# Sink values built one operation a step, and a narrower first query block

## The chip, the cores and the metric

The kernel runs on one core of a Trainium2 chip. The metric is the device time of one execution in microseconds (us). Five engines work side by side, each through its own queue in order: TensorE (PE; its weight loads are listed as PEld), VectorE (DVE), ScalarE (ACT), GpSimd (POOL), and SyncE (SP), which here only issues DMAs.

## The reference

Attention with a sliding window and sinks over 4 sequences, 8 heads, 768 positions and 64 dimensions, followed by a two-layer network over all 3072 tokens:

```
scores = q @ k.T / sqrt(64)
keep   = (key < 4) | (0 <= query - key < 128)        # sinks, window
a      = softmax(where(keep, scores, -1e9));  out = a @ v
x      = out of all heads side by side                # 3072 x 512
h      = x @ w_in                                     # 512 x 2048
g      = max(h, 0) + log1p(exp(-|h|))                 # softplus
result = g @ w_out                                    # 3072 x 512
```

## The kernel before

**Tiling.** A chunk is 256 queries of one sequence, two query blocks of 128 (j = 0 and 1). Three chunks make a sequence, so there are 12 chunks; chunks 0, 3, 6 and 9 are the first of their sequence (`self.first`). For each head and query block the scores are taken against the key block before it, 8 sink keys and its own key block: 128 + 8 + 128 = 264 columns. A predicated copy on VectorE (line 242) then lays the own block's kept scores (key not above the query) over those of the block before, so that 136 columns are left, 128 window keys and 8 sinks, to which a mask is added (line 248) and the exponential is taken on ScalarE (line 249). The host writes the first key block twice, so that the first query block of a sequence finds its own block also where the block before would stand; for it the copy writes values over equal ones.

**Precision.** Chunks 0 and 1 multiply in float32 (`exact`, scores at line 226). From chunk 2 on each operand is split into a rounded part in float32r (`hi`, fp32r in the profile) and a remainder, and a product is two or three matmuls in that type: the scores are hi x hi (line 229) and hi x remainder (line 230). So do the network's up product (line 459, 24 matmuls per 256 hidden units) and its down product (lines 496 to 498).

**Sink values.** The weights of the 8 sink keys are multiplied with the sinks' values in one matmul per head (line 327). Its stationary operand `vs` is built on POOL once per sequence for each group of 4 heads: after a DMA of the raw values (`load_sinks`, tile `vsr`), one operation rounds them (`vsh`, line 151), one takes the remainder in place (line 152), and for each group two operations place the rounded part and the remainder through a mask (line 158, tile `vs`). Six operations per sequence.

**Order.** In the main function the order of all engines is the order in which the program is written. A start phase is listed by hand (`START`). Then a loop runs over steps i, one head of attention each: while head i of the attention is finished, scores of head i+4 are made (S), softmax (T) and normalisation (N) of head i+4 follow, q, k and v of later heads are loaded and split (L, G, p, q), and for the network of the chunk before, one slice of 256 hidden units goes through up (U), softplus (F), gate (P), residue (R, a step later) and down (D, E, two steps later). W makes the transposed weights of head i and rearranges them on POOL into `pt` (lines 308, 311); V is the values' matmuls (lines 327, 333), which read `pt`. The gate's copy is POOL's rounding of softplus into `gh` (line 52), after VectorE's sum `mt` (line 474). The order of the letters in a step:

```
for part in "JjGL" + c.STEADY[i % H == 0]:
Ctx.STEADY = ("kWUqpKSFTRDVPONE", "SWTkpUKERDNFPqVO")
```

J and j build the sink values of the first and the second group of heads. J comes two steps ahead of a chunk's first step (chunk k begins at step 8k), at the head of the step, with the DMA and four POOL operations; j comes in step 8k+1, also at the head, with two operations. They run for the first chunk of each sequence and for chunk 2, the first one in the split form.

Of the kernel before, what the change touches and what calls it, by code (L numbers as in the profile page):

```python
# [12 lines left out]
F32R = mybir.dt.float32r  # L13
# [7 lines left out]
B, H, S, D = 4, 8, 768, 64  # L21
DM, DFF = 512, 2048
P = 128
NB = S // P
NS = 8
KW = P + NS
CH = 2
# [9 lines left out]
BIG = 3.0e38  # L37
G = 4
ORDERED = {mybir.EngineType.PE, mybir.EngineType.SP}


class Ctx:
# [80 lines left out]
class _Attention:  # L123
# [16 lines left out]
    def sinks(self, g):  # L140

        c, nc, b = self.c, self.c.nc, self.b
        raw = c.vsr[b]
        if self.exact:
            c.vs[b, g] = c.lp.tile([P, G, D], F32, tag=f"vsf{g}", name=f"vsf{g}", bufs=1)
            nc.gpsimd.memset(c.vs[b, g][:], 0.0)
            self._place(c.vs[b, g][:64], raw[:64, g : g + 1], 64)
            return
        if g == 0:
            c.vsh[b] = c.lp.tile([P, 2, D], F32R, tag="vsh", name=f"vsh{b}", bufs=1)  # L150
            nc.gpsimd.tensor_scalar(c.vsh[b][:], raw[:], 1.0, 0.0, ALU.mult, ALU.add)
            nc.gpsimd.tensor_tensor(raw[:], raw[:], c.vsh[b][:], ALU.subtract)
        c.vs[b, g] = c.lp.tile([P, G, P], F32R, tag=f"vs{g}", name=f"vs{b}_{g}", bufs=1)
        for src, o in ((c.vsh[b], 0), (raw, D)):
            self._place(c.vs[b, g][:, :, o : o + D], src[:, g : g + 1], P)

    def _place(self, out, src, rows):
        self.c.nc.gpsimd.tensor_tensor(
# [57 lines left out]
    def scores(self, h):  # L216
        c, nc = self.c, self.c.nc
        ops = self.heads.pop(h)
        for j in range(CH):
            pool, tag = (c.ps_h, "h") if self.chunk == 0 and h % 2 else (c.ps_s, "s")  # L220
            s = pool.tile([P, 2 * P + NS], F32, tag=tag, name=f"s{self.chunk}_{h}_{j}")
            mv = slice(j * KW, j * KW + 2 * P + NS)
            st = slice(KC + j * P, KC + j * P + P)
            if self.exact:
                q, k = ops
                nc.tensor.matmul(s[:], q[:, j * P : j * P + P], k[:, mv], start=True, stop=True)  # L226
            else:
                hi, kl = ops
                nc.tensor.matmul(s[:], hi[:, st], hi[:, mv], start=True, stop=False)  # L229
                nc.tensor.matmul(s[:], hi[:, st], kl[:, mv], start=False, stop=True)  # L230
            self.s[h, j] = s

    def softmax(self, h):
        c, nc, chunk = self.c, self.c.nc, self.chunk
        g, hh = h // G, h % G
        if hh == 0:
            self.a[g] = c.ap.tile([P, G, CH, KW], F32, tag="a", name=f"a{chunk}_{g}")
            self.rc[g] = c.sp.tile([P, CH, G], F32, tag="rc", name=f"rc{chunk}_{g}")
        sm = c.sp.tile([P, CH], F32, tag="sm", name=f"sm{chunk}_{h}")
        self.sm[h] = sm  # L240
        for j in range(CH):
            nc.vector.copy_predicated(self.s[h, j][:, :P], c.diag[:], self.s[h, j][:, KW:])  # L242
        for j in range(CH):
            a = self.a[g][:, hh, j]
            k = (chunk * H + h) * CH + j
            nm = c.stats[:, k : k + 1]
            m = c.masks[min(self.i0 + j, 2)]
            nc.vector.tensor_tensor_reduce(a, self.s.pop((h, j))[:, :KW], m[:], -SCALE, BIG, ALU.add, ALU.min, nm)  # L248
            nc.scalar.activation(a, a, AF.Exp, bias=nm, scale=-1.0, accum_out=sm[:, j : j + 1])  # L249
# [260 lines left out]
def _fast(c):  # L510
# [5 lines left out]
    n = c.nchunks  # L516
    att = [_Attention(c, k) for k in range(n)]
# [24 lines left out]
    def stage(kind):  # L542
        def run(i):
            if not todo[kind]:
                return
            o, e = todo[kind][0]
            before = "acdl"["acdl".index(kind) - 1]
            while kind != "a" and todo[before] and todo[before][0][0] <= o:
                stage(before)(i)
            home = _turn(c.WM, o)  # L550
            if kind == "a":
                while any(u is c.upper[c.turn] for u in c.top.values()):
                    stage("c")(i)
            elif kind == "c" and home == "p":
                while sum(_turn(c.WM, k) == "p" for k, _ in todo["l"] if k < o) > 1:
                    stage("l")(i)
            todo[kind].pop(0)
            if kind == "a":
                _weight_top(c, e, _turn(c.WT, o))
            elif kind == "c":  # L560
                _weight_f32(c, e, home)
            elif kind == "d":
                _weight_high(c, e, engine(c.WH, o))
            else:
                _weight_low(c, e, _turn(c.WL, o) if home == "s" else "V")

        return run
# [11 lines left out]
    def sinks(g):  # L579
        def run(i):  # L580
            k = (i - g * G) // H
            if (i - g * G) % H == 0 and k < n and (att[k].first or k == c.EXACT):
                if g == 0 and k:
                    att[k].load_sinks()
                att[k].sinks(g)

        return run

    parts = {
        "S": (call(att, "scores"), G),  # L590
# [15 lines left out]
        "G": (call(att, "load_v", 2), 2),  # L606
        "L": (call(att, "load"), G + 2),
        "J": (sinks(0), 2),
        "j": (sinks(1), G - 1),
        "w": (dma, 0),  # L610
        **{kind: (stage(kind), 0) for kind in "acdl"},
    }
# [183 lines left out]
def _kernel(tc, a, out):  # L796
# [7 lines left out]
    with ExitStack() as keep:  # L804
        c.const = keep.enter_context(tc.tile_pool(name="const", bufs=1))
        c.wp = keep.enter_context(tc.tile_pool(name="wp", bufs=1))
        c.w, c.raw, c.top, c.word = {}, {}, {}, {}
        c.ident = c.const.tile([P, P], F32, name="ident")
        c.stats = c.const.tile([P, B * H * NB], F32, name="stats")
        c.room = c.const.tile([P, 2, 4 * FP], F32, name="room")  # L810
        nc.gpsimd.memset(c.room[:], 1.0)
        c.sk = c.const.tile([P, CT], F32R, name="sk")
        ones = c.room[:].rearrange("p a b -> p (a b)").unsqueeze(1).broadcast_to([P, CT // 64, 64])
        _zero(nc, c.sk[:].rearrange("p (a b) -> p a b", b=64), ones)
        with ExitStack() as st:
            pool = lambda n, bufs: st.enter_context(tc.tile_pool(name=n, bufs=bufs))
            psum = lambda n, bufs: st.enter_context(tc.tile_pool(name=n, bufs=bufs, space=bass.MemoryType.PSUM))
            c.xp, c.mp, c.stg = pool("xp", 2), pool("mp", 2), pool("stg", 4)
            c.lp, c.ap, c.sp = pool("lp", 2), pool("ap", 2), pool("sp", 2)
            c.ps_acc, c.ps_h = psum("ps_acc", 1), psum("ps_h", 2)  # L820
            c.ps_s, c.ps_t, c.ps_x = psum("ps_s", 2), psum("ps_t", 1), psum("ps_x", 1)
            with tc.manual_schedule(engines=ORDERED):
                _fast(c)
        ok = nc.values_load(c.flag[:1, :1], min_val=0, max_val=1)
        with tc.If(ok < 1):
            _general(c)
# [8 lines left out]
Ctx.WT = "PAAVVVVAVAAVAAAVAAAAAAAAAAAPAAAV"  # L835
Ctx.WH = "VAPAAVAAAAVPPAAAAVVAVAAAAAVAVAAA"
Ctx.WL = "PPPPPPPVPPVPPVPPVPVPPPPVVPVVPVPV"
Ctx.STEADY = ("kWUqpKSFTRDVPONE", "SWTkpUKERDNFPqVO")
Ctx.START = """
S0 G4 T0 w w S1 j4 T1 J0 w L8 w w S3 S2 N0 N1 T2 W0 L10 w N2 S4 T3 N3 a w T4 k0 a c K0 a S5 c W1 w w  # L840
d S6 V0 O0 l d V1 w c l T5 N4 W2 T6 d w a S7 c O1 W3 l N5 G6 N6 a T7 c V2 N7 a d S8 k4 a O2 W4 w T8
# [62 lines left out]
```

## Time and profile before

| what | us |
|---|---|
| median of 3 runs (730.6 to 734.53) | 733.28 |
| the profiled execution | 729.99 |
| its span | 728.3 |
| TensorE busy in it | 695.7 |
| VectorE busy | 551.4 |
| ScalarE busy | 453.0 |
| POOL busy | 396.2 |

The span runs from the first to the last instruction of the profiled execution; its own time is a little longer. Busy is the time in which at least one instruction of the engine was under way. Matmuls overlap, so their pace is read from one start to the next and not from their duration. In lists of instructions a row gives the start in us from the beginning of the span, the duration, the engine, the line, the operation, the tile written and those read, the shape, the count, and in brackets the idle time of the engine before it and what ended that. A row of groups gives, after the bar, busy us and mean ns, and after the next bar idle us and who ended it. A row of waits gives us in total, times, and the longest. A row of stretches gives the stretch and its length, then for each engine the busy us with the number of instructions, the granted TensorE clock, and the DMA share and rate.

### The profile page before, as it was taken

To read this page: it belongs to the slowest core of one execution; us is meant where nothing else is said; L and a number is where in the kernel's file an instruction comes from. 1 tells how busy PE (TensorE), PEld (TensorE's weight loads), DVE (VectorE), ACT (ScalarE), POOL (GpSimd) and SP (SyncE) were. 2 spreads that over 40 slices of the span, in tenths; PEclk is the share of its full clock that TensorE was granted. 3 is DMA by queue.
4 is the path that set the end of the run, shared out by engine and by line. 5 is a ranking of instruction groups with operands and counts; after the bars stand their busy time and mean duration, and the time that the engine had idled before them with its cause. 6 is when DMAs were issued, how large, how long until landed. Compare 5 with 4: busy or idle time off the path is not lost.

```text
span 728.3 us, 13870 instructions
## 1 busy us (share of the span) xinstructions
PE 695.7 (96%) x4465; PEld 619.4 (85%) x4465; DVE 551.4 (76%) x1628; ACT 453.0 (62%) x1122; POOL 396.2 (54%) x769
## 2 busy tenths in 40 slices
PE   4888899999999999999999999999999999999996
PEld 3566689989999989988899999998899899999995
DVE  5899997877887887886977887886887877754331
ACT  3687865656676666765766766665766766744431
POOL 5766475575655655664664654656555565553110
PEclk9899999999999999999999999999999999999999
DMA  8888511411321321321222221321312312100001
GB/s 298 298 270 263 162 52 39 128 48 45 99 68 49 107 68 49 108 67 45 82 67 68 78 77 54 91 74 50 92 46 77 95 51 78 59 13 1 30 1 34
DMA packets 41205, 63.37 MB, mean 87 GB/s; under 512 B 4644, under 2 KB 22692, under 8 KB 41124
## 3 DMA queue, kind: packets, MB, share of 16 engines
q1 hardware_dynamic: 36372, 45.63, 21.4%
q10 hardware_dynamic: 4752, 16.77, 6.7%
q8 instruction: 37, 0.61, 0.4%
q14 instruction: 44, 0.36, 0.2%
HBM read 56.09 MB, written 6.29 MB: 86 GB/s over the span
## 4 chain that ended last, share of the span: by engine, by line
PE 83%; DVE 7%; POOL 3%; ACT 3%; issue 1%; DMA 1%; ACTq 0%; SPq 0%; POOLq 0%; DVEq 0%
PE h L459 33%; PE acc L496 11%; PE acc L497 11%; PE acc L498 11%; PE x L333 6%; PE s L229 2%; PE t L297 2%; PE s L230 2%; PE x L327 2%; PE s L226 2%; ACT a L249 1%; DVE wt L403 1%; DVE s L242 1%; POOL a L263 1%; POOL pt L308 1%
## 5 line engine op out<-in xcount | busy, mean ns | idle before, releaser
L459 PE MATMUL h<-xh,wi 128*128 128x256 f32 x1536 | 253.4, 287 | 0.0
L459 PEld LDWEIGHTS h<-xh,wi 128*128 128x128 f32 x1536 | 210.9, 191 | 1.1 <-issue 0.3
L459 PE MATMUL h<-xl,wi 128*128 128x256 f32 x768 | 154.5, 283 | 0.0
L496 PE MATMUL acc<-wo,gh 128*128 128x512 f32 x384 | 152.8, 398 | 0.0
L498 PE MATMUL acc<-wo,gl 128*128 128x512 f32 x384 | 151.0, 393 | 0.9 <-DVE gl L56 0.9
L52 POOL TENSOR_SCALAR gh<-mt 128x512 fp32r<-128x512 f32 x91 | 56.9, 626 | 173.8 <-DVE mt L474 147.8
L497 PE MATMUL acc<-wo,gh 128*128 128x512 f32 x384 | 150.8, 393 | 0.0
L466 ACT ACTIVATE mt<-h 128x512 f32<-128x512 f32 x96 | 57.5, 599 | 104.0 <-PE h L459 103.5
L263 POOL TENSOR_SCALAR a<-a,rc 128x128 f32<-128x128 f32 x180 | 71.9, 412 | 91.2 <-DVE rc L256 47.7
L459 PEld LDWEIGHTS h<-xl,wi 128*128 128x128 f32 x768 | 119.4, 191 | 0.0
L474 DVE SCALAR_TENSOR_TENSOR mt<-h,mt 128x512 f32<-128x512 f32 x96 | 65.8, 685 | 47.2 <-ACT mt L468 34.6
L249 ACT ACTIVATE a<-a,stats 128x136 f32<-128x136 f32 x192 | 76.0, 397 | 38.5 <-DVE stats L248 38.5
L498 PEld LDWEIGHTS acc<-wo,gl 128*128 128x128 f32 x384 | 72.2, 188 | 17.8 <-DVE gl L56 1.3
L496 PEld LDWEIGHTS acc<-wo,gh 128*128 128x128 f32 x384 | 72.4, 189 | 12.9 <-issue 0.5
L497 PEld LDWEIGHTS acc<-wo,gh 128*128 128x128 f32 x384 | 72.4, 189 | 9.4
L56 DVE TENSOR_TENSOR gl<-mt,gh 128x512 fp32r<-128x512 f32 x96 | 72.9, 759 | 4.9 <-POOL gh L52 4.6
L468 ACT ACTIVATE mt<-mt 128x512 f32<-128x512 f32 x96 | 60.8, 633 | 3.1
L467 ACT ACTIVATE mt<-mt 128x512 f32<-128x512 f32 x96 | 60.7, 633 | 3.1
L48 ACT CAST qkh<-qk 128x656 fp32r<-128x656 f32 x80 | 59.3, 741 | 1.2 <-DMA qk<-qk 1.2
L242 DVE COPY_PREDICATED s<-diag,s 128x128 f32<-128x128 int32 x192 | 48.6, 289 | 14.5 <-PE s L230 11.3
L56 DVE TENSOR_TENSOR kl<-qk,qkh 128x400 fp32r<-128x400 f32 x80 | 52.3, 654 | 2.5
L333 PE MATMUL x<-pt,vv 128*128 128x256 f32 (+1 forms) x216 | 48.9, 328 | 4.7 <-POOL pt L311 4.7
(182 smaller groups left out, 1207.7 us busy)
## 6 DMA issues: line engine op xcount, KB each, us to landing
qk<-qk SPq DMA_DIRECT2D x160, 164.0 KB, 3.0
vr<-v SPq DMA_DIRECT2D x32, 192.0 KB, 2.7
out<-o SPq DMA_DIRECT2D x24, 256.0 KB, 2.1
q<-q SPq DMA_DIRECT2D x8, 256.0 KB, 4.9
vr<-v SPq DMA_DIRECT2D x16, 128.0 KB, 2.2
k<-k SPq DMA_DIRECT2D x8, 200.0 KB, 4.7
wi00r<-w ACTq DMA_DIRECT2D x1, 511.8 KB
wi01r<-w ACTq DMA_DIRECT2D x1, 511.8 KB
```

The source lines that it names most:

```text
L48: nc.scalar.copy(out, in_)
L56: (nc.vector if eng == "V" else nc.gpsimd).tensor_tensor(out, a, b, ALU.subtract)
L249: nc.scalar.activation(a, a, AF.Exp, bias=nm, scale=-1.0, accum_out=sm[:, j : j + 1])
L263: (nc.vector if eng == "V" else nc.gpsimd).tensor_scalar(a, a, rc[:, j : j + 1], 0.0, ALU.mult, ALU.add)
L333: nc.tensor.matmul(x[:, :, o], w, pt[:, :, m], start=False, stop=n == 2, skip_group_check=True)
L459: nc.tensor.matmul(h[:, j], wt, x, start=k == 0, stop=k >= len(prods) - 2, skip_group_check=True)
L467: nc.scalar.activation(t[:], t[:], AF.Exp, scale=-1.0)
L468: nc.scalar.activation(t[:], t[:], AF.Ln, bias=1.0)
L474: nc.vector.scalar_tensor_tensor(t[:], h[:], 0.0, t[:], ALU.max, ALU.add)
L496: nc.tensor.matmul(acc[:], gh[:, j, q], wh, start=f == 0, stop=False, skip_group_check=True)
L497: nc.tensor.matmul(acc[:], gh[:, j, q], wl, start=False, stop=False, skip_group_check=True)
L498: nc.tensor.matmul(acc[:], gl[:, j, q], wh, start=False, stop=f == 2 * FP - 1, skip_group_check=True)
```

## The change

**Sink values.** J and j stay for chunk 0 and chunk 2 alone. For chunks 3, 6 and 9 a new letter Y does the same work in single pieces, at a place behind q (the split of v) and ahead of P (the gate): in step 8k-6 the DMA, in -4 the rounding, in -3 the remainder, in -2 and -1 the first group's two placings, in +1 and +2 the second group's. None falls on a step divisible by 8.

**Scores.** The first query block of a sequence takes 136 columns, its own key block (where the block before stands otherwise) and the sinks, and has no predicated copy. This holds for chunks 0, 3, 6 and 9, in both precisions.

```diff
+SINK_STEPS = {
+    -6: ("load_sinks",),
+    -4: ("sink_split", 0),
+    -3: ("sink_split", 1),
+    -2: ("sink_half", 0, 0),
+    -1: ("sink_half", 0, 1),
+    1: ("sink_half", 1, 0),
+    2: ("sink_half", 1, 1),
+}
...
+    def sink_split(self, e):
+        c, nc, b = self.c, self.c.nc, self.b
+        raw = c.vsr[b]
+        if e == 0:
             c.vsh[b] = c.lp.tile([P, 2, D], F32R, tag="vsh", name=f"vsh{b}", bufs=1)
             nc.gpsimd.tensor_scalar(c.vsh[b][:], raw[:], 1.0, 0.0, ALU.mult, ALU.add)
+        else:
             nc.gpsimd.tensor_tensor(raw[:], raw[:], c.vsh[b][:], ALU.subtract)
...
+    def sink_half(self, g, e):
+        c, b = self.c, self.b
+        if e == 0:
+            c.vs[b, g] = c.lp.tile([P, G, P], F32R, tag=f"vs{g}", name=f"vs{b}_{g}", bufs=1)
+        src, o = ((c.vsh[b], 0), (c.vsr[b], D))[e]
+        self._place(c.vs[b, g][:, :, o : o + D], src[:, g : g + 1], P)
...
-            mv = slice(j * KW, j * KW + 2 * P + NS)
+            w = KW if self.first and j == 0 else 2 * P + NS
+            mv = slice(j * KW, j * KW + w)
             st = slice(KC + j * P, KC + j * P + P)
+            o = s[:, :w]
...
-                nc.tensor.matmul(s[:], hi[:, st], hi[:, mv], start=True, stop=False)
-                nc.tensor.matmul(s[:], hi[:, st], kl[:, mv], start=False, stop=True)
+                nc.tensor.matmul(o, hi[:, st], hi[:, mv], start=True, stop=False)
+                nc.tensor.matmul(o, hi[:, st], kl[:, mv], start=False, stop=True)
...
-        for j in range(CH):
+        for j in range(1 if self.first else 0, CH):
             nc.vector.copy_predicated(self.s[h, j][:, :P], c.diag[:], self.s[h, j][:, KW:])
...
-            if (i - g * G) % H == 0 and k < n and (att[k].first or k == c.EXACT):
+            if (i - g * G) % H == 0 and k in (0, c.EXACT):
...
+    def next_sinks(i):
+        for k in range(c.EXACT + 1, n):
+            if att[k].first and i - k * H in SINK_STEPS:
+                what, *args = SINK_STEPS[i - k * H]
+                getattr(att[k], what)(*args)
...
+        "Y": (next_sinks, 0),
...
-Ctx.STEADY = ("kWUqpKSFTRDVPONE", "SWTkpUKERDNFPqVO")
+Ctx.STEADY = ("kWUqYpKSFTRDVPONE", "SWTkpUKERDNFPqYVO")
```

More of the change, by code (lines that the diff above doesn't have):

```diff
@@ L149, in sinks @@
         if g == 0:
+            self.sink_split(0)
+            self.sink_split(1)
+        for e in range(2):
+            self.sink_half(g, e)
+    def sink_split(self, e):
+        c, nc, b = self.c, self.c.nc, self.b
+        raw = c.vsr[b]
+        if e == 0:
             c.vsh[b] = c.lp.tile([P, 2, D], F32R, tag="vsh", name=f"vsh{b}", bufs=1)
             nc.gpsimd.tensor_scalar(c.vsh[b][:], raw[:], 1.0, 0.0, ALU.mult, ALU.add)
+        else:
             nc.gpsimd.tensor_tensor(raw[:], raw[:], c.vsh[b][:], ALU.subtract)
-        c.vs[b, g] = c.lp.tile([P, G, P], F32R, tag=f"vs{g}", name=f"vs{b}_{g}", bufs=1)
-        for src, o in ((c.vsh[b], 0), (raw, D)):
-            self._place(c.vs[b, g][:, :, o : o + D], src[:, g : g + 1], P)
+    def sink_half(self, g, e):
[4 more added lines that the diff above has]
+        self._place(c.vs[b, g][:, :, o : o + D], src[:, g : g + 1], P)
     def _place(self, out, src, rows):
@@ L221, in scores @@
             s = pool.tile([P, 2 * P + NS], F32, tag=tag, name=f"s{self.chunk}_{h}_{j}")
-            mv = slice(j * KW, j * KW + 2 * P + NS)
+            w = KW if self.first and j == 0 else 2 * P + NS
+            mv = slice(j * KW, j * KW + w)
             st = slice(KC + j * P, KC + j * P + P)
+            o = s[:, :w]
             if self.exact:
                 q, k = ops
-                nc.tensor.matmul(s[:], q[:, j * P : j * P + P], k[:, mv], start=True, stop=True)
+                nc.tensor.matmul(o, q[:, j * P : j * P + P], k[:, mv], start=True, stop=True)
             else:
                 hi, kl = ops
-                nc.tensor.matmul(s[:], hi[:, st], hi[:, mv], start=True, stop=False)
-                nc.tensor.matmul(s[:], hi[:, st], kl[:, mv], start=False, stop=True)
+                nc.tensor.matmul(o, hi[:, st], hi[:, mv], start=True, stop=False)
+                nc.tensor.matmul(o, hi[:, st], kl[:, mv], start=False, stop=True)
             self.s[h, j] = s
```

## The prediction

> **What bounds the kernel now.** I read the page's busy shares first, then the busy time of the engines by stretches, then the stretch of one step of the loop in order of time.
>
> ```profile
> PE 695.7 (96%) x4465; PEld 619.4 (85%) x4465; DVE 551.4 (76%) x1628; ACT 453.0 (62%) x1122; POOL 396.2 (54%) x769
> ```
>
> TensorE is busy for 96% of the span. Where the rest lies is told by stretches (length, then busy time of each engine):
>
> ```profile
> core 0: us, PE busy (x) PEld busy (x) DVE busy (x) ACT busy (x) POOL busy (x), PEclk, DMA share, GB/s
> 111.73:617.40 505.67, 500.93 (x3310) 455.59 (x3308) 407.49 (x1213) 332.92 (x836) 292.58 (x585) 1.00 0.25 71
> 0.00:111.73 111.73, 90.86 (x498) 70.19 (x499) 96.58 (x291) 73.51 (x189) 70.91 (x120) 0.95 0.68 222
> ```
>
> From 111.73 us on TensorE leaves only 505.67 - 500.93 = 4.74 us idle; before that it is idle for 20.9 us, VectorE is the busiest engine and the granted clock is below 1. So there are two regimes: a start ruled by dependences, and a loop in which time is what TensorE executes plus 4.74 us. The waits say what these are:
>
> ```profile
> PE x L333 <- POOL pt L311: 6.5, 4, 1.8
> ```
>
> Four waits of the values' matmuls for the rearranged weights `pt`; one is in the start. The other three fall into the steps two ahead of chunks 3, 6 and 9, where a new sequence's sink values are built. Each is set beside a step of the same kind three chunks or one chunk away:
>
> ```profile
> 153.12:161.90 8.78, 7.22 (x49) 6.31 (x48) 5.49 (x17) 4.43 (x11) 6.61 (x13) 1.00 0.29 81
> 265.86:272.79 6.93, 6.93 (x49) 6.31 (x48) 4.97 (x16) 4.43 (x11) 4.32 (x9) 1.00 0.39 116
> ...
> 490.29:499.07 8.78, 7.22 (x49) 6.31 (x48) 5.48 (x17) 4.43 (x11) 6.61 (x13) 1.00 0.27 81
> 603.04:609.98 6.94, 6.94 (x50) 6.33 (x48) 4.93 (x16) 4.44 (x11) 4.26 (x9) 1.00 0.42 112
> ```
>
> 8.78 against 6.93 us, with TensorE short of work only there and POOL at 6.61 us instead of 4.3, with 13 instructions instead of 9. POOL's order of time in the first of them shows why (gh is the gate's copy of the step before, then of this one):
>
> ```profile
> 152.79 0.62 POOL L52 TENSOR_SCALAR gh<-mt 128x512 fp32r<-128x512 f32 x1 [1.31 <-DVE mt L474]
> ...
> 155.55 0.60 POOL L151 TENSOR_SCALAR vsh<-vsr 128x128 fp32r<-128x128 f32 x1
> 156.24 0.46 POOL L152 TENSOR_TENSOR vsr<-vsr,vsh 128x128 f32<-128x128 f32 x1
> 156.66 0.61 POOL L158 TENSOR_TENSOR vs<-vsh,hmask 128x256 fp32r<-128x256 f32 x1
> 157.23 0.61 POOL L158 TENSOR_TENSOR vs<-vsr,hmask 128x256 fp32r<-128x256 f32 x1
> 157.80 0.86 POOL L308 TENSOR_SCALAR_AFFINE_SELECT pt<-th 128x256 fp32r<-128x256 f32 x1
> ...
> 159.33 0.40 POOL L311 TENSOR_SCALAR_AFFINE_SELECT pt<-tl 128x256 fp32r<-128x256 f32 x1
> 159.72 0.62 POOL L52 TENSOR_SCALAR gh<-mt 128x512 fp32r<-128x512 f32 x1
> ```
>
> ```profile
> 159.79 0.39 PE L333 MATMUL x<-pt,vv 128*128 128x256 f32 x1 [1.56 <-POOL pt L311]
> ```
>
> The four sink operations stand in POOL's queue from 155.55 to 157.80, 2.25 us, ahead of `pt`; TensorE waits 1.56 us for the last `pt`, and restarting makes the step 1.85 us longer.
>
> **The change, part by part.**
>
> *The burst.* Nothing is taken away: per new sequence the six operations (0.60 + 0.46 + 4 x 0.61 = 3.5 us) are issued one by one in steps -4, -3, -2, -1, +1 and +2 around its first chunk, behind the values' split and ahead of the gate's copy, no longer ahead of `pt`. TensorE's wait goes: 3 x 1.85 = 5.5 us. The slack of `pt` without the burst is about 2.25 - 1.85 = 0.4 us, so a remainder would need POOL to be late from the step before. What covers each moved operation is POOL's idle time in front of the gate's copy:
>
> ```profile
> POOL gh L52 <- DVE mt L474: 147.8, 72, 5.7
> ```
>
> ```profile
> 182.79 0.62 POOL L52 TENSOR_SCALAR gh<-mt 128x512 fp32r<-128x512 f32 x1 [1.34 <-DVE mt L474]
> ```
>
> The copy waits 147.8 / 72 = 2.1 us in the mean for VectorE's sum; the tightest of chunk 3's steps are -3 (1.31 us, at 152.79 above) and +1 (1.34), against 0.46 to 0.61 us each; in step -2 `pt` ends 2.25 us earlier than shown, which is the cover. All hidden, cost 0; with the cover gone an operation costs up to its 0.61 us. Queued behind it are the gate's copy, then VectorE's residue, then the down matmuls of two steps later, so the copy may itself slip some. In step +1 two operations leave the place ahead of `pt`; no wait is seen there now, so nothing is counted. The DMA of the sink values moves from the head of step -2 to the middle of step -6 in SP's queue, behind that step's loads; the first reader stands two steps, some 14 us, later. Behind it in SP's queue wait the next step's loads, and SP would stop only if POOL had not read the last sequence's values: these reads lie some 16 steps back ahead of chunks 6 and 9, and one step back ahead of chunk 3. Cost 0; without that cover, a part of one step at chunk 3.
>
> *136 columns in the loop.* Three chunks x 8 heads x 2 products = 48 short matmuls in the rounded type fp32r, on the bounding engine. Now:
>
> ```profile
> 156.07 0.29 PE L229 MATMUL s<-qkh 128*128 128x264 f32 x1
> 156.19 0.29 PE L230 MATMUL s<-kl,qkh 128*128 128x264 f32 x1
> ...
> 156.56 0.39 PE L496 MATMUL acc<-wo,gh 128*128 128x512 f32 x1
> 156.79 0.39 PE L497 MATMUL acc<-wo,gh 128*128 128x512 f32 x1
> ```
>
> Start to start: 0.12 us for 264 columns, 0.23 us for 512, so 0.44 ns a column. No fp32r matmul of the trace has under 256 columns, so the price is bounded. From below, by columns alone: 0.122 - 128 x 0.00044 = 0.066 us, a gain of 48 x 0.056 = 2.7 us. But each matmul has a weight load of its own, and right after the wait, with no matmul to hold it back, the loads come at this distance:
>
> ```profile
> 159.79 0.19 PEld L333 LDWEIGHTS x<-pt,vv 128*128 128x128 f32 x1 [1.88 <-POOL pt L311]
> 159.89 0.19 PEld L333 LDWEIGHTS x<-pt,vv 128*128 128x128 f32 x1
> ```
>
> 0.10 to 0.11 us a load: at 136 columns the load would set the pace, at about 0.11 us, and 48 x 0.01 = 0.5 us is gained. From above, the only 4-byte matmuls in the trace that are not rounded, the first two chunks' scores, of which each is two records:
>
> ```profile
> 31.47 1.13 PE L226 MATMUL s<-k,q 128*128 128x264 f32 x4 [1.09 <-DVE stats L248]
> 31.99 0.39 PE L226 MATMUL s<-k,q 128*128 128x264 f32 x1
> 32.43 0.27 PE L279 MATMUL ts<-ident,sa 128*64 128x128 f32 x1
> ```
>
> The record at 31.99 (of a narrower stretch) is the third of the four, so two take 0.44 us: a whole matmul of 264 columns costs 0.44 us, four times the rounded one, and 136 columns would cost 0.23 us. If a short rounded matmul fell back to that rate, it would lose 48 x (0.23 - 0.12) = 5.2 us. I take 0.11 us: the load's row is of the very same kind (128x128 weights, same type), the other is of another type.
>
> The Trainium skill, page "FP8 and Floating Point Precision", TensorE Precision Notes, says that true FP32 takes four passes through the array and reduced FP32 is read as 4 bytes and cut to the native width. That fits 0.44 against 0.12 us here, and it makes the passes a matter of type, not of columns, which speaks against the 5.2 us; no run here shows a short one.
>
> *No self-copy.* 24 copies leave VectorE in the loop; it is not the bound there (407 of 506 us), so 0, covered by TensorE. The score banks and exponentials come earlier by one copy, which no one waits for.
>
> *The start (chunk 0).* Eight matmuls of 16 records shrink to 136/264, and 8 copies go. Here the chain that ended last runs through them:
>
> ```profile
> by line: PE s L226 31.1%; DMA q<-q 14.3%; ACT a L249 8.0%; issue 6.5%; DVE s L242 4.8%; DVE sm L255 4.2%; PE x L327 3.7%; PE x L333 3.5%; DVE a L248 3.0%; DVE wt L403 2.8%; DVE rc L256 2.8%; PE t L297 2.7%; DVE upper L50 2.4%; DVE th L50 1.
> ...
> 5.72 3.78 PE s L226 x8
> 10.13 2.03 PE s L226 x8
> ...
> 18.04 1.76 PE s L226 x4
> 20.23 1.76 PE s L226 x4
> ```
>
> This is the chain within the first 30 us: 31.1%, 9.3 us, are chunk 0's score records, 4.8%, 1.4 us, its copies. Half of both are of the first query block; its records lose 48% (4.7 x 0.48 = 2.2 us), its copies all (0.7 us): at most 2.9 us. Some of it will be met by exponentials that stay on the way. On the other side, the granted clock is 0.95 in the mean there (stretches above): a record takes 0.44 us at 5.72, 18.04 and 20.23, twice the 0.22 us at 31.99. A changed start may meet the slow stretches with other work; two more pieces like those of 1.76 us would lose 0.9 us each, 1.8 us. Between -2.9 and +1.8 I take -2.0, nearer to the chain's own rows.
>
> **Sum.** -5.5 - 0.5 - 2.0 = -8.0 us. The profiled execution took 729.99 us (span 728.3), 3.3 under the median of 733.28: 722.0 by its own time, 725.3 against the median, a gain of 1.1%. I give times against the median. About 0.5%, 3.7 us, is what a measurement of this kernel can tell from no change: its three runs lie 730.6 to 734.53.
>
> **Rivals.**
> 1. Short rounded matmuls run at the unrounded rate, 0.23 us. For it: nothing in the kernel goes below 256 columns in this type, so the single rate is only known there. Against: the weight load's row. -5.5 + 5.2 - 2.0 = -2.3: 731.0 us, no change to be told.
> 2. Columns set the pace, 0.066 us, since weight loads overlap better than the row suggests. Against: two loads 0.10 to 0.11 us apart with TensorE free. -5.5 - 2.7 - 2.0 = -10.2: 723.1 us. The Trainium skill, "TensorE: Matmul & The Clock Gate", Back-to-back issue gap, gives about 81 ns a matmul for sustained pairs of load and matmul at 128 columns; by that estimate the term would be 48 x 0.04 = 1.9 us instead of 0.5. The trace's 0.10 to 0.11 us is longer, and decides.
> 3. The other side: the sink operations now delay the gate's copy. Place: the six steps around chunks 3, 6, 9. Price: all 3.5 us exposed three times, 10.5 us, in place of the 5.5: -8.0 + 10.5 = +2.5, 735.8 us. It decides, against the whole gain, once three quarters of the operations are exposed. Against it: the idle times of 1.31 us and more above.
> 4. The start gives nothing back, or the wait at `pt` only halves (the work before it is late in the odd steps): -6.0 or -5.2, 727.3 to 728 us. Still faster; inside my case's range.
>
> **How the numbers follow.** My case with rival 4: 0.55, own range 722 to 729. Rival 1: 0.30. Rival 2: 0.06. Rival 3: 0.05. The remaining 0.04 is a short matmul dearer than rival 1's; slower from 0.122 + 7.5 / 48 = 0.28 us. Faster by over 0.5% (under 729.6): 0.52 of my case, 0.08 of rival 1, all 0.06 of rival 2, together 0.66. Slower by over 0.5% (above 737): 0.02 each of rivals 1 and 3 and of the rest, 0.06. Same: 0.28. The range 721 to 732.5 leaves out a quarter of rival 1, rival 3, the rest and a little below: under 0.2.
>
> **What would show it.** In the changed profile: the wait of x L333 for POOL pt falls from four to one in the waits; the steps before chunks 3, 6, 9 take 6.9 us; the score rows of 128x136 have starts 0.11 us apart (0.23 for rival 1, seen as two records or as 0.1 us more in each of eight steps; 0.07 for rival 2); POOL's gate copy still waits for VectorE's mt in those steps; the stretch up to the first up matmul of chunk 1 (111.73 us now) gets about 2 us shorter. A price of the short matmul above 0.2 us, or a new wait for gl or gh, makes the prediction wrong.

## The result, and the profile after

The changed kernel takes 722.83 us (median of 4 runs, 722.06 to 723.8) against 733.13 us for the kernel before beside it (730.6 to 734.53): a ratio of 0.9875, 95% interval 0.9852 to 0.9899. The 725.3 us of the prediction lie 2.5 us above, the range 721 to 732.5 holds the time. In the comparison below with more runs of the kernel before, the same kernel comes to 0.9886 (0.9863 to 0.9909). The medians differ by 10.3 us (7.4 to 10.9 us by the interval). Profile against profile it is 722.06 against 729.99 us, a difference of 7.9 us, and the predicted sum was 8.0. The terms fit less well than that, as the stretches show. First the changed kernel, loop (first up matmul of chunk 1 to that of chunk 11), start, end, then the step ahead of chunk 3 (those ahead of chunks 6 and 9 take 6.94 and 6.93 us):

```profile
110.97:663.58 552.61, 552.59 (x3658) 503.51 (x3656) 437.06 (x1277) 363.19 (x906) 323.47 (x641) 1.00 0.23 68
0.00:110.97 110.97, 89.70 (x499) 69.71 (x499) 95.91 (x283) 73.37 (x189) 71.14 (x120) 0.95 0.68 224
663.58:720.36 56.78, 50.65 (x314) 45.33 (x312) 16.05 (x37) 16.51 (x27) 5.19 (x9) 0.99 0.06 21
152.34:159.28 6.94, 6.94 (x50) 6.32 (x48) 5.11 (x15) 4.44 (x11) 4.96 (x10) 1.00 0.36 101
```

The loop and the end of the kernel before (its start, 111.73 us, stands in the prediction):

```profile
111.73:670.68 558.95, 554.21 (x3658) 503.90 (x3657) 438.83 (x1301) 362.99 (x906) 320.08 (x641) 1.00 0.23 67
...
670.68:728.28 57.60, 50.65 (x314) 45.34 (x312) 16.04 (x37) 16.51 (x27) 5.17 (x9) 0.98 0.06 20
```

The loop lost 6.34 us, the start 0.76, the end 0.82. By the profile TensorE is now busy all through the loop, 552.59 of 552.61 us. That does not mean that nothing is left to gain: the last experiment takes another 1.28 us out of it. In the waits of the changed kernel, of four waits of the values' matmuls one is left, that of the start:

```profile
PE x L362 <- POOL pt L340: 1.9, 1, 1.9
```

POOL's order around chunk 3 in the changed kernel, steps -4, -3 and +1:

```profile
142.55 0.30 POOL L172 TENSOR_SCALAR vsh<-vsr 128x128 fp32r<-128x128 f32 x1
145.35 0.63 POOL L63 TENSOR_SCALAR gh<-mt 128x512 fp32r<-128x512 f32 x1 [2.50 <-PE acc L526]
...
150.70 0.91 POOL L174 TENSOR_TENSOR vsr<-vsr,vsh 128x128 f32<-128x128 f32 x1
152.05 0.62 POOL L63 TENSOR_SCALAR gh<-mt 128x512 fp32r<-128x512 f32 x1 [0.45 <-DVE mt L503]
...
178.54 1.06 POOL L185 TENSOR_TENSOR vs<-vsh,hmask 128x256 fp32r<-128x256 f32 x1
179.89 0.62 POOL L63 TENSOR_SCALAR gh<-mt 128x512 fp32r<-128x512 f32 x1 [0.29 <-DVE mt L503]
```

Each of these operations ends before what the gate's copy waits for, which is VectorE's sum, and in step -4 a down matmul. The tightest places are those that the prediction named. In step -3 the remainder takes 0.91 us instead of 0.46, and 0.45 us of idle time is left; in step +1 the placing takes 1.06 us instead of 0.61, and 0.29 us is left. The three other steps leave 1.3 us. And the short matmuls of the changed kernel, in step -3 of chunk 3, up to the first of the values' matmuls:

```profile
148.38 0.23 PE L258 MATMUL s<-qkh 128*128 128x136 f32 x1
148.44 0.27 PE L259 MATMUL s<-kl,qkh 128*128 128x136 f32 x1
148.55 0.34 PE L258 MATMUL s<-qkh 128*128 128x264 f32 x1
148.73 0.29 PE L259 MATMUL s<-kl,qkh 128*128 128x264 f32 x1
148.85 0.40 PE L525 MATMUL acc<-wo,gh 128*128 128x512 f32 x1
...
150.25 0.28 PE L356 MATMUL x<-sk,vs 128*128 128x256 f32 x1
```

The weight loads there:

```profile
148.38 0.19 PEld L259 LDWEIGHTS s<-kl,qkh 128*128 128x128 f32 x1
148.49 0.19 PEld L258 LDWEIGHTS s<-qkh 128*128 128x128 f32 x1
```

Each is one record. The first lets its follower start after 0.06 us, but the matmul after that comes 0.11 us later and the long ones are held up: the four take 0.47 us from 148.38 to 148.85, where four of 264 columns take 0.49 (156.07 to 156.56 before). The loads stand 0.11 us apart. So the short matmul costs about 0.11 us at this place, as taken. But in this step what it saves is gone six matmuls later. The same step in the kernel before:

```profile
149.14 0.28 PE L229 MATMUL s<-qkh 128*128 128x264 f32 x1
...
149.64 0.40 PE L496 MATMUL acc<-wo,gh 128*128 128x512 f32 x1
...
151.01 0.28 PE L327 MATMUL x<-sk,vs 128*128 128x256 f32 x1
```

The four score matmuls take 0.50 us there and the six down matmuls behind them 1.37; in the changed kernel they take 0.47 and 1.40. Both sums are 1.87 us. Steps -1, +1 and +3 do the same; steps -2 and +2 keep the saving.

### The profile page after: what moved, and what is told of

Its sections match the earlier page's. It is cut to its first block, busy times and chain, and to the rows that moved or that the text cites. A ratio compares the mean times of both kernels' runs of the same rounds, so it can differ in the third digit from the quotient of the medians.

```text
span 720.4 us, 13834 instructions
## 1 busy us (share of the span) xinstructions
PE 692.9 (96%) x4465; PEld 618.6 (86%) x4465; DVE 549.0 (76%) x1596; ACT 453.1 (63%) x1122; POOL 399.8 (56%) x769
## 4 chain that ended last, share of the span: by engine, by line
PE 90%; DVE 3%; ACT 2%; DMA 2%; POOL 1%; issue 1%; SPq 0%; ACTq 0%; POOLq 0%
PE h L488 37%; PE acc L525 12%; PE acc L527 12%; PE acc L526 12%; PE x L362 6%; PE t L326 3%; PE s L258 3%; PE s L259 3%; PE x L356 2%; DMA wo71r<-w 1%; DMA q<-q 1%; ACT a L278 1%; DVE sm L284 1%; DMA words<-sizes 1%; DVE wt L432 0%
## 5 line engine op out<-in xcount | busy, mean ns | idle before, releaser
L67 DVE TENSOR_TENSOR gl<-mt,gh 128x512 fp32r<-128x512 f32 x96 | 76.6, 798 | 4.9 <-POOL gh L63 4.6
L271 DVE COPY_PREDICATED s<-diag,s 128x128 f32<-128x128 int32 x160 | 41.8, 290 | 15.4 <-PE s L259 12.5
L337 POOL TENSOR_SCALAR_AFFINE_SELECT pt<-th 128x256 fp32r<-128x256 f32 (+1 forms) x96 | 46.6, 486 | 8.0 <-DVE th L61 5.0
```

The lines of the kernel that those rows point to most:

```text
L67: (nc.vector if eng == "V" else nc.gpsimd).tensor_tensor(out, a, b, ALU.subtract)
```

## The experiments

Theory: the loop's gain is the burst that no longer stands ahead of `pt`, plus a little for the short matmuls; the start gives up to 2 us. Rival: the scores carry the gain, since the first medians moved by more than the loop did. Each kernel ran beside runs of the kernel before on the same chip, one profile each. All numbers together:

| kernel | ratio to before (95%) | loop us | first up matmul of all at us | chunk 1's first up at us |
|---|---|---|---|---|
| before, second profile | 1.0018 (1.0004 to 1.0033) | 558.99 | 41.56 | 112.66 |
| changed, again | 0.9886 (0.9863 to 0.9909) | 552.61 | 41.27 | 112.19 |
| sink values only | 0.9938 (0.9916 to 0.9960) | 553.22 | 41.96 | 113.13 |
| scores only | 0.9965 (0.9949 to 0.9980) | 558.18 | 41.24 | 112.36 |
| burst behind pt | 0.9886 (0.9864 to 0.9908) | 552.49 | 41.29 | 112.40 |
| 200 columns | 0.9877 (0.9856 to 0.9898) | 552.30 | 41.35 | 112.28 |
| chunk 0 only | 0.9972 (0.9958 to 0.9986) | 558.90 | 41.94 | 112.09 |
| no copy only | 0.9996 (0.9982 to 1.0011) | 558.34 | 41.14 | 111.28 |
| changed, early matmuls | 0.9893 (0.9876 to 0.9911) | 552.55 | 40.10 | 111.66 |
| the same, checks behind 8k+7 | 0.9963 (0.9949 to 0.9978) | 558.58 | 40.78 | 110.94 |
| before, early matmuls | 0.9978 (0.9965 to 0.9992) | 559.17 | 40.51 | 111.38 |
| changed, checks behind 8k+2, 4, 6 | 0.9854 (0.9828 to 0.9880) | 551.33 | 40.05 | 110.98 |

The second run of the kernel before shows how far a ratio can be trusted: 0.2% for an identical kernel. The first profiles had the first up matmul at 41.84 us before and 40.05 us after. The loop is the finer measure: where its code is the same it takes 558.90 to 559.17 us in four profiles (the kernel before twice, chunk 0 only, before with early matmuls) and 552.55 to 552.61 us in three (the change twice, and with early matmuls). A difference under 0.3 us between two loops is therefore weak unless it stands in the same steps of every chunk.

**Sink values only.** Of the change, the new steps and the letter Y; `w`, `o` and the shorter range of the copy are left out:

```diff
-            w = KW if self.first and j == 0 else 2 * P + NS
-            mv = slice(j * KW, j * KW + w)
+            mv = slice(j * KW, j * KW + 2 * P + NS)
...
-        for j in range(1 if self.first else 0, CH):
+        for j in range(CH):
```

> The sink values are spread as in the change; the first query block keeps 264 columns and its copy. Theory (the burst ahead of pt is the main cost): the waits of the values' matmuls for pt that stood in the steps ahead of chunks 3, 6 and 9 go, those steps fall from 8.78 to 6.93 us, and the steps behind (8k+1) lose another 0.2 us, in all -6.2 us in the loop; the start (first up matmul of chunk 1 at 111.7 us) does not move; the time is 0.8% below before, ratio 0.9915. Rival (the scores carry the gain, since the medians moved by 10 us and the spans by 8): under 4 us, ratio above 0.9945.

The loop is 5.7 us shorter (553.22 against 558.95). The step ahead of chunk 3 falls to 6.94 us; the step 8k+1 behind it falls less than expected, from 7.01 to 6.96 (stretches of this kernel):

```profile
154.51:161.45 6.94, 6.94 (x49) 6.33 (x48) 5.28 (x16) 4.44 (x11) 4.92 (x10) 1.00 0.35 103
...
175.31:182.27 6.96, 6.96 (x48) 6.20 (x47) 6.23 (x17) 5.42 (x13) 4.94 (x9) 1.00 0.11 31
```

The rival falls: nine tenths of the loop's gain are here. The ratio, 0.9938, is weaker than the 0.9922 that 5.73 us of loop alone would give, but its interval holds that.

**Scores only.** The other half of the change, on the kernel before.

> 136 columns and no self-copy in the first query block, sink values built in bursts as before. Theory: three waits for pt of about 1.56 us stay; the four score matmuls of a first-chunk step take 0.47 instead of 0.495 us from their first start to the next matmul, -0.6 us in the loop; the first up matmul (41.8 us before) comes about 1.8 us earlier, of which 0.8 to 1.8 us arrives at chunk 1 (111.7 us before): -1.4 to -2.4 us in all, ratio 0.9967 to 0.998. Rival (scores carry the gain): -4 us or more, ratio under 0.9945.

The loop gives 0.8 us, the time 2.6 us (0.35%): close to the size the theory had, but, as the kernel without copies shows below, 0.6 us of the 0.8 are the copies' and not the columns'. The first up matmul of all comes at 41.24 us, 0.6 us earlier and not 1.8. The burst's step stays at 8.79 us. Step 8k+1 is 6.84 us here. The two halves of the loop add up to 6.5 us, the change has 6.34.

**Burst behind pt.** The place of the change, but not its spread:

```diff
-    -4: ("sink_split", 0),
-    -3: ("sink_split", 1),
-    -2: ("sink_half", 0, 0),
-    -1: ("sink_half", 0, 1),
-    1: ("sink_half", 1, 0),
-    2: ("sink_half", 1, 1),
+    -2: (("sink_split", 0), ("sink_split", 1), ("sink_half", 0, 0), ("sink_half", 0, 1)),
+    1: (("sink_half", 1, 0), ("sink_half", 1, 1)),
```

> As the change, but the four operations of the first group stand together in step 8k-2 and the two of the second in step 8k+1, at the same place, behind pt and ahead of the gate's copy. Theory of the place (what costs is to stand ahead of pt): TensorE's steps stay at 6.93 us, only the gate's copy on POOL comes up to 0.7 us later, which the down matmuls two steps later don't see; the time is that of the change within 0.3%. Theory of the spread (a burst costs wherever it stands, since gh, gl or the next pt come late): the step or the one after grows by 0.5 to 1.9 us, 1.5 to 5.5 us in all, ratio to before 0.990 to 0.995.

The place decides, not the spread. In this kernel the four operations run in a row and hold the gate's copy up, and no one waits for that:

```profile
157.60 0.41 POOL L336 TENSOR_SCALAR_AFFINE_SELECT pt<-tl 128x256 fp32r<-128x256 f32 x1
157.98 0.30 POOL L168 TENSOR_SCALAR vsh<-vsr 128x128 fp32r<-128x128 f32 x1
...
159.67 0.61 POOL L181 TENSOR_TENSOR vs<-vsr,hmask 128x256 fp32r<-128x256 f32 x1
160.26 0.62 POOL L59 TENSOR_SCALAR gh<-mt 128x512 fp32r<-128x512 f32 x1
```

The copy has no idle time in front of it any more and starts 6.50 us into the step instead of 6.16 in the change, the step still takes 6.93 us, and the loop, 552.49 us, is that of the change. This kernel and the change both also move the DMA of the raw values to step -6, and no run tries that alone. In the kernel before, POOL has no idle time ahead of the rounding at 155.55 us, so nobody waited for that DMA.

**200 columns.**

```diff
-            w = KW if self.first and j == 0 else 2 * P + NS
+            w = (KW if self.exact else 200) if self.first and j == 0 else 2 * P + NS
```

> The changed kernel, but the rounded scores of the first query block take 200 columns instead of 136 (64 more, unused); chunk 0 stays at 136. In the changed kernel the four score matmuls of such a step take 0.469 us from the first start to the next matmul, against 0.495 us with 264 columns. Theory (the weight load sets the pace of a short matmul): 0.47 us again, loads 0.11 us apart, the loop as in the changed kernel within 0.2 us. Rival (the price falls with the columns): in between, 0.482 us if it is a straight line from 264 to 136.

```profile
149.69 0.26 PE L258 MATMUL s<-qkh 128*128 128x200 f32 x1
149.79 0.27 PE L259 MATMUL s<-kl,qkh 128*128 128x200 f32 x1
149.90 0.30 PE L258 MATMUL s<-qkh 128*128 128x264 f32 x1
150.04 0.28 PE L259 MATMUL s<-kl,qkh 128*128 128x264 f32 x1
150.16 0.39 PE L525 MATMUL acc<-wo,gh 128*128 128x512 f32 x1
...
151.52 0.28 PE L356 MATMUL x<-sk,vs 128*128 128x256 f32 x1
```

149.69 to 150.16 is 0.47 us, the same as with 136: 64 columns more cost nothing. Between 136 and 200 columns the matmul is not paid by the column. The loads stand 0.11 us apart in the change, so the load's pace is the likely price; no run changes the load itself. The loop, 552.30 us, is even 0.31 us shorter than with 136, more than the 0.2 us that was allowed for, and by the same amounts in the same steps around chunks 3, 6 and 9. The rows show where: the six down matmuls behind take 1.36 us (150.16 to 151.52), not 1.40.

**Chunk 0 only, no copy only, and the kernel before again.** The first two are edits of the kernel before:

```diff
+            w = KW if self.chunk == 0 and j == 0 else 2 * P + NS      # chunk 0 only
...
+        for j in range(1 if self.chunk == 0 else 0, CH):              # chunk 0 only
...
+        for j in range(1 if self.first else 0, CH):                   # no copy only
```

> The kernel before, with 136 columns and no self-copy in chunk 0 alone. Theory (the start's share is real but shared out by half-clock stretches): the loop from the first up matmul of chunk 1 to that of chunk 11 takes 558.9 us as before; the time is 1 to 2.5 us lower, ratio 0.9965 to 0.9985. Rival (what chunk 0 saves is given back before the loop, as in the first profile, 0.8 us): ratio above 0.9985.

> The kernel before without the predicated copy of the first query block, all matmuls at 264 columns. Theory (VectorE is not the bound in the loop, and in the start the copies are the smaller part, 0.7 us at most): loop unchanged within 0.2 us, ratio 0.999 to 1.0. Rival (the copies are what helped in the start): ratio 0.9965 to 0.998.

> The kernel before itself, for a second profile of its start. Theory: the loop takes 558.9 us again, the start differs from 111.7 us by up to 1.5 us with the place of the half-clock stretches; ratio 1.000 within 0.002.

Chunk 0 alone gives 2.0 us (1.0 to 3.1) by the ratio and leaves the loop alone, as expected; but its profile has chunk 1's first up at 112.09 us, inside what the kernel before shows (111.73, 112.66). Removing the copies alone gives no time that can be told from none, but it does shorten the loop by 0.6 us, against the expectation of 0.2 at most. All of it is in the three steps 8k+1 of the first chunks. The first of them in the kernel before (the others take 7.07 and 7.03 us), and in the kernel without the copies (6.85 and 6.84):

```profile
175.76:182.77 7.01, 7.01 (x48) 6.19 (x47) 6.28 (x17) 5.41 (x13) 4.93 (x10) 1.00 0.11 32
```

```profile
175.31:182.11 6.80, 6.80 (x48) 6.19 (x47) 6.28 (x16) 5.21 (x13) 4.90 (x10) 1.00 0.07 23
```

TensorE counts as busy in all of both, and VectorE's busy time, 6.28 us, is the same, so busy time does not tell the cause. The waits of TensorE's weight loads for `pt` do; in the kernel before, without the copies, in the change, and with the checks behind 8k+2, 4 and 6:

```profile
PEld x L333 <- POOL pt L311: 10.1, 12, 2.3
```

```profile
PEld x L333 <- POOL pt L311: 9.3, 9, 2.3
```

```profile
PEld x L362 <- POOL pt L340: 3.7, 6, 2.3
```

```profile
PEld x L362 <- POOL pt L340: 2.3, 1, 2.3
```

Of the twelve, one is in the start, three are the bursts, and eight stand in steps 8k+1: three in those of chunks 3, 6 and 9, five in those of chunks 4, 5, 7, 8 and 10. Without the copies the three are gone. In the kernel before the chain to `pt` in these three steps runs through the copies: in step 8k they delay the exponentials on ScalarE by 0.2 us, with them the softplus behind, then VectorE's sum, the gate's copy and the two placings on POOL, and `pt`:

```profile
176.39 0.69 DVE L474 SCALAR_TENSOR_TENSOR mt<-h,mt 128x512 f32<-128x512 f32 x1 [0.66 <-ACT mt L468]
...
177.24 0.62 POOL L52 TENSOR_SCALAR gh<-mt 128x512 fp32r<-128x512 f32 x1 [0.59 <-DVE mt L474]
```

The sum starts 0.63 us into the step; without the copies 0.43. Where the placings are moved away and the copies stay (sink values only), `pt` waits 0.97 us for VectorE's remainder `tl` instead, so that kernel gained little in these steps.

**The changed kernel again.**

> The changed kernel once more beside the others. Theory: the loop gives -6.8 us always; what is over that is made in the start, by where the half-clock stretches of TensorE fall; the ratio lies at 0.9865 to 0.990, and the profile's steps from 111 us on are those of the first profile within 0.05 us, while the moment of the first up matmul of chunk 1 can differ by 1 us or more.

The loop repeats, with a gain of 6.34 us and not the 6.8 of the theory. The start is 1.2 us longer than in the first profile, and the first rows of scores tell why. TensorE's first matmuls, in the kernel before (second profile), in the changed kernel (second profile), in the changed kernel (first profile):

```profile
5.60 3.64 PE L226 MATMUL s<-k,q 128*128 128x264 f32 x8 [5.60 <-DMA q<-q]
9.88 2.02 PE L226 MATMUL s<-k,q 128*128 128x264 f32 x8 [0.65 <-PE s L226]
```

```profile
5.64 3.01 PE L255 MATMUL s<-k,q 128*128 128x136 f32 x8 [5.64 <-DMA q<-q]
9.24 3.04 PE L255 MATMUL s<-k,q 128*128 128x136 f32 x8 [0.60 <-DVE stats L277]
```

```profile
9.26 1.67 PE L255 MATMUL s<-k,q 128*128 128x136 f32 x8 [0.60 <-DVE stats L277]
```

The same eight records take 3.04 us in one profile and 1.67 us in the other: half clock against full clock. With 264 columns the second group ran at full clock (2.02 us) in every profile. With 136 columns and no early matmuls the first group lasts 3.0 instead of 3.6 to 3.9 us, and in five of seven profiles the full clock was granted only at 13.5 to 14.4 us. In the two where it was granted at 9.2 to 9.3 us, the first up matmul of all comes at 40.05 us and chunk 1 starts at 110.97 and 110.98 us; in the five, at 41.2 to 41.9 and 112.1 to 112.4. The Trainium skill, "TensorE: Matmul & The Clock Gate", Part 1, says that the full clock needs about 3.4 us of sustained work in a window that runs free of the kernel, so that the moment varies from run to run. The trace fits that: 3.6 us of work and more got the full clock early in four of four profiles, 3.0 us in two of seven.

**Early matmuls.** Eight matmuls of the identity, ahead of everything in TensorE's queue, on the changed kernel and on the kernel before; the third kernel also moves VectorE's weight checks.

```diff
+def _warm(c, n):
+    w = c.ps_x.tile([P, P], F32, tag="x", name="warm")
+    for _ in range(n):
+        c.nc.tensor.matmul(w[:], c.ident[:], c.ident[:], start=True, stop=True)
...
         _constants(c)
+        _warm(c, 8)
...
-            if i >= 2 * H + lag and i % 2 == 0 and checks:
+            if i >= 2 * H + lag and i % H in (2, 4, 6, 7) and checks:      # third kernel
```

> The changed kernel with eight matmuls of the identity by itself (128x128, float32, result not read) in TensorE's queue ahead of the first scores, where TensorE otherwise waits for q until 5.6 us. In five of six profiles with 136 columns in chunk 0 the full clock is granted at 13.5 to 14.4 us, not at about 9.3 as with 264. Theory (the shorter first scores are too little work for the clock, and that takes back what they save): with the idle time filled the full clock comes by 9.3 us or sooner, the scores of heads 2 to 4 run at 0.12 and 0.22 us a record, and the first up matmul comes 1 to 2 us before the 41.3 us of the changed kernel; ratio to before 0.985 to 0.988. Rival (the clock is not what holds the start: DMA and exponentials do): first up matmul at 41 us or later, ratio as for the change, 0.9886.

> The kernel before with the same eight matmuls. Theory: the first scores at 264 columns then run at full clock too, so the first up matmul comes 0.5 to 2 us before 41.7; ratio 0.997 to 0.9995, and what 136 columns in chunk 0 bring is smaller than without. Rival: no change, 1.000.

> As e7_warm, and the weight checks on VectorE (line 469) are made behind the steps 8k+2, +4, +6 and +7 instead of behind every even step. Theory: in steps 8k+1 of the later chunks (7.08 to 7.22 us against 6.93) pt waits for VectorE's remainder tl, which stands behind the two checks of the step before; moved away, these steps take 6.93 us and the loop of 552.6 us loses about 1.2 us; ratio to before 0.9835 to 0.987. Rival (VectorE is not what delays tl): loop unchanged.

The full clock comes earlier, as expected; the gain doesn't follow. With the early matmuls the changed kernel's first scores run at full clock halfway through:

```profile
2.30 3.79 PE L543 MATMUL warm<-ident 128*128 128x128 f32 x16 [2.30 <-POOL ident masks.py:199]
5.88 1.98 PE L255 MATMUL s<-k,q 128*128 128x136 f32 x8
8.46 1.67 PE L255 MATMUL s<-k,q 128*128 128x136 f32 x8 [0.60 <-DVE stats L277]
```

1.98 instead of 3.01 us, and the first up matmul of all comes at 40.1 instead of 41.3 us. But chunk 1 starts at 111.66 us, only 0.5 earlier, and the ratio, 0.9893, is that of the change: the expected 0.985 to 0.988 was missed. From the first up matmul to chunk 1's this kernel takes 71.56 us, the longest of all profiles (70.92 in both of the change); why is not shown. On the kernel before, the early matmuls give 0.2%, no more than a repeated kernel shows.

Moving the checks went wrong in an instructive way. Steps 8k+1 of the later chunks did fall (7.19 to 6.92 us), but the steps before them rose from 6.55 to 7.58 us:

```profile
222.14:229.72 7.58, 6.97 (x46) 5.91 (x45) 5.53 (x20) 3.76 (x11) 2.17 (x6) 1.00 0.10 34
```

```profile
225.80 0.27 PE L308 MATMUL ts<-ident,sa 128*64 128x128 f32 x1 [0.54 <-DVE sa L297]
```

Behind step 8k+7 the check's two operations stand ahead of VectorE's sink weights, for which TensorE waits at once. The loop got 6 us longer.

**Checks behind 8k+2, 4 and 6.** On the changed kernel without the early matmuls.

```diff
-            if i >= 2 * H + lag and i % 2 == 0 and checks:
+            if i >= 2 * H + lag and i % H in (2, 4, 6) and checks:
```

> The changed kernel (without the matmuls of the identity), with the weight checks behind steps 8k+2, +4 and +6 only; those left over come at the end. Behind 8k+7 they made the steps 8k of the later chunks 0.8 to 1.0 us longer, since the sink weights sa stand behind them; behind 8k+8 they made 8k+1 longer. Theory (VectorE's place is what counts): steps 8k as in the changed kernel (6.43 to 6.56 us), steps 8k+1 at 6.93 us or less, the loop of 552.6 us shorter by about 1.2 us, the end unchanged within 0.5 us; ratio to before 0.985 to 0.988. Rival: steps 8k+1 stay at 7.1 to 7.2 us, or the end grows by as much.

```profile
110.98:662.31 551.33, 551.33 (x3658) 503.53 (x3656) 435.43 (x1273) 362.13 (x906) 323.08 (x641) 1.00 0.23 68
...
221.39:227.94 6.55, 6.55 (x46) 5.99 (x45) 4.51 (x18) 3.87 (x12) 2.17 (x6) 1.00 0.14 45
227.94:234.86 6.92, 6.92 (x50) 6.33 (x48) 6.05 (x16) 5.43 (x13) 4.84 (x9) 1.00 0.09 25
```

The loop is 1.28 us shorter than the change's, with both steps at their best, and no wait of the weight loads for `pt` is left in it. The time is 721.96 us, ratio 0.9854 (0.9828 to 0.9880): the best of all, and clearly ahead of the kernel before. Ahead of the change it is by the loop alone; the ratios overlap.

## Why the prediction was right, point by point

**The burst (-5.5).** Right, mechanism and size: (8.78 + 8.77 + 8.78) - (6.94 + 6.94 + 6.93) = 5.52 us, and the sink values alone take 5.7 us off the loop. That spreading was needed is refuted: at the new place the whole burst is hidden. Rival 3 asked what happens if the gate's copy is held up; in that kernel it is, by 0.3 us, and the down matmuls two steps later don't notice. The cover is therefore larger than the idle time that the prediction named; how much larger wasn't tried.

**136 columns in the loop (-0.5).** The price of a matmul was right, and so was "48 x 0.01" where these matmuls stand: in the 24 groups of four around chunks 3, 6 and 9, from the first start to the next matmul, they take 12.06 us before and 11.51 after, 0.55 us less. What failed is that the loop would lose as much. The six down matmuls behind 21 of the groups take 29.01 us before and 29.32 after (28.81 with 200 columns). So the loop is 558.18 us with scores only and 558.34 with the copies removed only: 0.16 us are left for the columns, a third of the term and within what loops of the same code differ by. With 200 columns the loop is 0.31 us shorter again. Why the shortest matmuls slow those behind them stays open. Rival 1, the unrounded rate, and rival 2, pay by the column, are both out: four matmuls would have taken 0.70 and 0.38 us. The weight load's row, from right after a wait, was the one to read. The estimate from the 81 ns of the Trainium skill's "TensorE: Matmul & The Clock Gate" for 128 columns would have given some 0.41 us for the four; 0.47 was measured.

**No self-copy (0 in the loop).** Wrong by 0.6 us. The steps that failed are "it is not the bound there (407 of 506 us), so 0", a mean over the loop, and that no one waits for the earlier exponentials. In the steps 8k+1 of the first chunks TensorE's weight loads waited for a `pt` at the end of a chain that began with the copies. The prediction read the four waits of the matmuls and saw none in step +1; the weight loads' row, with twelve, would have told, and so would the step's length against the 6.8 us of those around it. With the small relief from the burst these steps lost (7.01 + 7.07 + 7.03) - (6.81 + 6.81 + 6.82) = 0.67 us.

**The start (-2.0).** The mechanism was there, the size was not: -0.76 us in the first pair of profiles. In that pair the first up matmul of all comes 1.79 us earlier (41.84 to 40.05). From there to chunk 1's the kernel before and the change take:

```profile
41.84:111.73 69.89, 63.06 (x383) 51.72 (x383) 65.99 (x157) 51.76 (x114) 41.80 (x56) 0.98 0.56 178
```

```profile
40.05:110.97 70.92, 64.42 (x384) 52.99 (x383) 66.03 (x157) 51.62 (x114) 41.79 (x56) 0.95 0.55 174
```

So 1.03 us are lost again, at a granted clock of 0.95 instead of 0.98. This part does not go with chunk 0's columns: it takes 69.9 to 70.2 us at 0.98 in four profiles and 70.9 to 71.6 us at 0.95 in the ten others, and both widths stand in both groups. In this pair it was bad luck. Over all profiles the gain is small too. The seven profiles with chunk 0 at 136 columns and without early matmuls begin chunk 1 at 110.97 to 112.40 us, in the mean 111.9; three with 264 and the copy at 111.73, 112.66 and 113.13, in the mean 112.5: about 0.6 us. (With 264 columns and no copies it is 111.28 us in the one profile, so these few profiles do not part columns from copies.) The timed runs of chunk 0 alone say 2.0 us, with an interval from 1.0 to 3.1; in its profile 0.7 us of that are the end's. What eats the gain in five of the seven is the loss that the prediction had as its other end: the first full clock comes later, and the first up matmul of all at 41.2 to 41.9 us instead of 40.05, against 41.6 to 42.0 with 264 columns. That less work makes it later is argued from these counts and from the early matmuls, not tried by itself.

**The end (not in the sum).** 0.82 us, 57.60 to 56.78. All matmuls and copies of the end fall in the same places to 0.01 us; the difference is in the closing, after the last output is issued. It goes with chunk 0's 136 columns (0.3 to 0.8 us in all profiles of kernels with them and without early matmuls, none in those with 264), which have no visible tie to it. The cause wasn't tried and stays open.

So the sum of 8.0 met 7.9 in part by chance: the start's shortfall of 1.2 us was made up by 0.8 us at the end and 0.3 us more in the loop, where the copies gave more than the columns fell short.

## What to carry to other kernels

Where one engine's matmuls fill a step, look for the steps that are longer than their neighbours. Here each named a place where another queue had an item ahead of what that engine waits for, and moving the item behind it gained all, without spreading or shrinking it. Busy shares hide this, TensorE's own too; read the waits of its weight loads beside those of its matmuls. And what a few narrower matmuls save is to be read at the end of the step, not behind the last of them: here the matmuls that followed took more than half of it back.

## What the runs showed of the hardware that was not expected

- Less work at the beginning can cost clock: with the first eight records cut from 3.64 to 3.01 us, the full clock came some 4 us later in five of seven profiles, and the next eight took 3.04 instead of 1.67 us. In these stretches the clock column of the profile says 1.00 before the first change it recorded; the distance of the records is the surer sign.
- A matmul in the rounded type with 136 or 200 columns is one record and costs about 0.11 us with a weight load of its own, hardly less than 0.12 us with 264. Behind two of 136 and two of 264 columns the six matmuls of 512 columns took 1.40 us in step -3, behind four of 264 columns 1.37, behind two of 200 and two of 264 columns 1.36.
- On POOL the same remainder took 0.46 us in one place and 0.91 us in another, the rounding 0.60 and 0.30 us, the placing 0.61 and 1.06 us.
